# A two-layer Fourier and MLP kernel in float32: w3 and raw w4 loads at later steps, one product moved, norms a slot behind additions, six places for w4 tiles

## The chip, the cores and the metric

The kernel runs on one core of a Trainium2 chip. The metric is the device time of one execution, in microseconds (us). The engines of the core are named as in the profile: PE (TensorE, matrix products), DVE (VectorE), ACT (ScalarE), POOL (GpSimd) and SP (SyncE, which here issues all DMAs).

## The reference

The input `x` has 2048 tokens of 512 features, in float32. Two layers are computed, each in two sublayers that add to `x`:

```python
x = x + fourier(layernorm(x))      # Real(DFT_seq(DFT_hidden(.)))
x = x + mlp(layernorm(x))

def mlp(x):
    h  = gelu(layernorm(x) @ w1)            # 512 x 512
    hs = shift_tokens(h) @ w2               # four feature quarters by +1, -1, +2, -2
    x1 = x + hs
    return x1 + gelu(layernorm(x1) @ w3) @ w4   # 512 -> 1376 -> 512
```

## The kernel before

**Numbers and products.** Each float32 operand is split into a high part (a cast on ACT) and a low part (a subtraction on DVE); a product is three matmuls, high by high, high by low, low by high (`mm3`, lines 305 to 307). So every operand costs an ACT cast and a DVE "low" before TensorE can use it, and all three matmul lines look alike in the profile.

**Tiles.** The tokens stand in four chunks of 512 (`NC`), a chunk in four tiles of 128. The 1376 hidden features make eleven tiles (`NF`), numbered `fs` = 10, 0, 1, ... 9. Chunks 0 and 1 are worked as one pair, chunks 2 and 3 as the second. For h = gelu(z w3), two feature tiles and two chunks are a block product of 2 by 2, done in seven products instead of eight (`prod`, line 771) with sums of blocks named "11", "21", "12", "22", "t1" to "t4". Five such steps (p = 0 to 4) cover feature tiles 0 to 9; tile 10 is done by itself before (`w3x`).

**First pair** (in `by_pairs`, from line 1413). Each step p: seven products; two w4 tiles of the step before (`w4_part`, twelve matmuls each) for chunk c1; then after the last step two more tiles, and eleven tiles for chunk c2 (line 1532). w4 tiles come into six places `w4r`; after each tile the load that follows six tiles later is issued (`w4_load`). In layer 0 the steps also prepare the weights for all later uses (`w_prep`, line 1449): sums of w3, high and low parts, and stores of them in DRAM (`w3d`, `w3e`, `w4a`). Work that isn't bound to a place, the norms and transposes of chunks 2 and 3 for the second pair (z3), stands in a list `bg`, of which one entry, a slot, is run at each call of `one()`: two slots before step 0, two in step 0 and three in each later step of layer 0. The last entry stores z3 of chunk 3 (`turn_out`, line 616, four DMAs), and four loads (`b_in`, line 764) bring z3 back as blocks.

**Bank reuse in a step.** Block 11's product goes to bank b1; ACT copies it to `u` (line 1473); only then may block 21's product add to the same bank. Product t3 goes to bank b7, which is the bank b5 of the step before; there the last reader was that step's last addition.

**Second pair, layer 0** (`second_pair`, line 1286). Again tile 10, five steps and then 22 w4 tiles (eleven for each chunk). Beside the steps the first layer's raw w4 is brought in (`q4_raw`), summed for layer 1 (`q4_sums`, DVE, then a cast on ACT), its lows taken (`q4_lows`, DVE) and stored (`q4_keep`, DMA). These stand at five points of a step (`work`, line 1325). The w4 tiles come through six places `wq`, of which places 0 and 1 are used once. During the last eleven tiles the next layer's DFT blocks are brought into four places `raw` (`more`, line 1311) and made ready (`ahead`, line 289).

**Order.** The schedule is by hand: each engine runs its instructions in the order in which the program gives them, SP's DMAs among them. A DMA whose wait isn't over holds up all DMAs behind it on SP.

Of the kernel before, what the change touches and what calls it, by code (L numbers as in the profile page):

```python
# [8 lines left out]
F32 = mybir.dt.float32  # L9
# [25 lines left out]
WARM = 12  # L35

X6, X7 = 2, 4
HAT = (2, 3, 3, 4, 5, 5, 6, 6)
BACK = {1: (0,), 2: (2,), 6: (4,)}
HORDER = ((1, 0), (0, 1), (1, 1), (0, 0))  # L40
# [3 lines left out]
def spectral_mlp_kernel(ctx: ExitStack, tc: tile.TileContext, x, ws, hs, w1, w2, w34, out, out_t):  # L44
# [80 lines left out]
    extra = [at(f"extra{i}", EXT + i * D, D, dtype=F32) for i in range(6)]  # L125
    rest = [at(f"rest{i}", RAWS + i * D, D, dtype=F32) for i in range(8)]

    w4c, w4cf = zip(*(both(f"w4c{i}", word, 2, 4, 2 * P) for i, word in enumerate((6 * AY, 7 * AY, RNG))))
    w4raw = [at(f"w4raw{i}", RAWS + i * 2 * CH, 2, CH, dtype=F32) for i in range(2)]
    row_at = [ZW + i * CH for i in range(NF + 4)] + [RR + (8 + i) * CH for i in range(NF - 4)]  # L130
    hrow = [at(f"hrow{i}", word, CH, dtype=F32) for i, word in enumerate(row_at)]
    wq_at = [4 * CH, 6 * CH] + [RR + i * 2 * CH for i in range(4)]
    wq = [at(f"wq{i}", word, 2, CH) for i, word in enumerate(wq_at)]
    hp_at = [STG] + [RNG + (8 + 2 * i) * CH for i in range(3)] + [EXT + 2 * i * CH for i in range(3)]
    hp = [at(f"hp{i}", word, 2, CH) for i, word in enumerate(hp_at)]
# [647 lines left out]
            nc.sync.dma_start(to[:, 0], w34[NF - 1 + LAG, :, 1])  # L783

    def q4_sums(n):
        lo, w = w4cf[n % 3][:, 1], w4c[n % 3]
        (a11, a21), (a12, a22) = ([w4raw[n % 2][:, f, e * 2 * P : (e + 1) * 2 * P] for e in range(2)] for f in range(2))
        if n < NF // 2:
            add(lo[:, 1], a21, a22)
            add(lo[:, 3], a11, a21, ALU.subtract)  # L790
            add(lo[:, 2], lo[:, 1], a11, ALU.subtract)
            add(lo[:, 0], a12, lo[:, 2], ALU.subtract)
            nc.scalar.copy(w[:, 0], lo)
        else:
            add(lo[:, 0], a11, a21, ALU.subtract)
            add(lo[:, 1], a21, a11, ALU.subtract)
            nc.scalar.copy(w[:, 0, 0:2], lo[:, 0:2])

    def q4_lows(n):
        w, lo, u = w4c[n % 3], w4cf[n % 3][:, 1], slice(0, 4 if n < NF // 2 else 2)  # L800
        nc.vector.tensor_tensor(w[:, 1, u], lo[:, u], w[:, 0, u].bitcast(F32), op=ALU.subtract)

    def q4_keep(n):
        w = w4c[n % 3].bitcast(F32)
        if n < NF // 2:
            nc.sync.dma_start(w4s[:, n], w)
        else:
            nc.sync.dma_start(w4e, w[:, :, 0:2])

    def by_pairs(layer, zs, xin, dst):  # L810
# [147 lines left out]

        def w3_keep(n):
            nc.sync.dma_start(w3d[n], w3b[n % 2].bitcast(F32))  # L960

        sc0, sc1, sc2 = scratch
        for c in range(NC):
# [322 lines left out]
        def second_pair():  # L1286
# [19 lines left out]
                    nc.sync.dma_start(w_of(m).bitcast(F32), w4d[tiles[m][1]])  # L1306

            def w_of(m):
                return wq[m if m < 2 else 2 + (m - 2) % 4]

            def more():
                state.update(limit=w_items[1], load=len(pieces))
                issue_dma()

            s = w3xs[1][0]
            for c, names in ((c1, ("11", "21")), (c2, ("12", "22"))):
# [7 lines left out]

            def work(p):
                todo = {
                    0: [lambda: q4_sums(p)],
                    1: [lambda: xp_stats(p)] if p < half - 1 else [lambda: split_of(1)],
                    2: [lambda: q4_lows(p)],
                    3: [lambda: xp_norm_in(p)] if p < half - 1 else [lambda: split_of(2)],  # L1330
                    4: [lambda: q4_keep(p), lambda: q4_raw(p + 2) if p + 2 <= half else None],
                }
                if p == 1:
                    todo[3].append(lambda: split_of(0))
                if p == half - 1:
                    todo[2] += [lambda: load(0), lambda: load(1)]
                    todo[4].append(lambda: split_of(3))
                return todo

# [36 lines left out]
            def store(c):  # L1376
# [7 lines left out]
                NF: [lambda: drain(c1, acc4), lambda: store(c1)],  # L1384
                NF + 1: [lambda: xp_stats(4)],
                NF + 2: [lambda: xp_stats(5), lambda: xp_norm_in(4)],
                NF + 3: [lambda: xp_norm_in(5), more],
            }
            for m in (NF + 5, NF + 7, NF + 9):
                plan[m] = [lambda: ahead(1)]  # L1390
            for k, first in enumerate((0, 3, 6, 9, NF + 3, NF + 6)):
                for i, f in enumerate((xp_sums, xp_highs, xp_lows)):
                    plan.setdefault(first + i, []).append(lambda f=f, k=k: f(k))

            for m, (c, f) in enumerate(tiles):
                if m == NF:
                    for g in plan.pop(m):
                        g()
                acc, h, w = acc4 if c == c1 else mm4, splits.pop(m), w_of(m)
                split_of(m + 3) if m else None  # L1400
                for q in range(TC):
                    v = slice(q * P, (q + 1) * P)
                    mm3(acc[q], h[:, 0, v], h[:, 1, v], w[:, 0], w[:, 1], f == fs[0], f == fs[-1])
                if m >= 2:
                    load(m + 4)
                for g in plan.pop(m, ()):
                    g()
            assert not plan
# [4 lines left out]
        for pair in range(NC // 2):  # L1413
# [4 lines left out]
            bk, acc1 = (mm4, acc4) if pair == 0 else (acc4, mm4)  # L1418
            acc2 = [bk[i] for i in (3, 0, 1, 2)]
            if pair == 0:  # L1420
                bg += [] if layer else [lambda: None] * 2 + [u_stats(2, 0), u_stats(2, 2)]
                bg += [finish(2, 0), finish(2, 2), turn3(turned, 2, 0, 1), turn3(turned, 2, 2, 3)]
                bg += [lambda: turn_out(turned, z3d[2])]
                z3_last = lambda t: [
                    *(u_stats(3, 0), u_stats(3, 2), finish(3, 0), finish(3, 2)),
                    *(turn3(t, 3, 0, 1), lambda: (turn3(t, 3, 2, 3)(), turn_out(t, z3d[3]))),
                ]
                bg += z3_last(turned if layer else tmp[:, 0:4])
            tmps[:] = gs
            lows("t4")()  # L1430
            if layer == 0:
# [17 lines left out]
            def w_prep(p):  # L1449

                n, i = p + 1, 2 * p + 1
                w4_lows = lambda: (w4_low(i), w4_low(i + 1))
                w4_highs = lambda: (w4_high(i), w4_high(i + 1))
                if n == NF // 2:
                    return {1: [w4_highs], 5: [w4_lows]}
                return {
                    0: [lambda: w3_sums(n, 0), lambda: w3_highs(n, 1, 2)],
                    1: [lambda: w3_sums(n, 1), lambda: w3_highs(n, 0)],
                    2: [lambda: w3_lows(n, 1, 2), *([lambda: w3_load(n + 1)] if n < NF // 2 - 1 else [])],
                    3: [w4_highs],  # L1460
                    4: [lambda: w3_lows(n, 0), lambda: w3_keep(n)],
                    5: [w4_lows],
                }

            b1, b6, b5, b7 = bk[2], bk[3], bk[0], bk[1]
            for p in range(NF // 2):
                prep = {} if layer else w_prep(p)
                u, v, x, y = sets[p % 2]
                w = w3b[(5 * pair + p) % 2]
                if p:  # L1470
                    b1, b5, b7 = b7, b1, b5
                prod(b1, w, 4, "11")
                nc.scalar.copy(u, b1)
                at_point(0)
                prod(b6, w, 1, "t2")
                add(x, u, b6)
                prod(b5, w, 0, "t1")
                if layer:
                    one()
                at_point(1)  # L1480
                prod(b1, w, 5, "21", True)
                low1 = gelu_high(h4[2 * (p % 2)], b1)
                at_point(2)
                prod(b7, w, 2, "t3")
                add(v, x, b7)
                add(y, v, b5)
                gelu(hc[:, 2 * p + 1], y)
                if layer:
                    one()
                low1()  # L1490
                at_point(3)
                tiles = [(fs[0], h4[2])] if p == 0 else [(2 * p - 2 + i, h4[2 * ((p - 1) % 2) + i]) for i in range(2)]
                for i, (f, h) in enumerate(tiles):
                    w4_part(acc1, f, h, lambda: at_point(4 + i))
                    w4_load()
                    one()
                at_point(4)
                at_point(5)
                if p == NF // 2 - 1:
                    split_later(0)  # L1500
                    split_later(1)
                prod(b1, w, 6, "t4")
                add(v, v, b1)
                low2 = gelu_high(h4[2 * (p % 2) + 1], v)
                prod(b5, w, 3, "22", True)
                add(x, x, b5)
                low2()
                gelu(hc[:, 2 * p], x)
                at_point(6)
                if layer or p >= NF // 2 - 2:  # L1510
                    w3_load(5 * pair + p + 2)
                one()

            if pair == 0:
# [2 lines left out]
                        b_in(c, half, to)  # L1517
                bg += [sum_of("t1", "12", "11"), sum_of("t2", "22", "t1"), sum_of("t3", "22", "12"), sum_of("t4", "21", "t2")]
                bg += [parts(b) for b in ("11", "21", "12", "22", "t2", "t1", "t3", "t4")]
            if layer == 0:  # L1520
                nc.sync.dma_start(w3xs[1][0].bitcast(F32), w3e)
                q4_raw(0)
                q4_raw(1)
            for i in range(2):
                w4_part(acc1, NF - 3 + i, h4[i])
                w4_load()
# [5 lines left out]
            for k in range(NF):  # L1532
                w4_part(acc2, fs[k], h4[(2 + k) % 4])
                w4_load()
                if k:
                    split_later(k + 3)
                one()
            drain(c2, acc2)
            for j in range(c2 * TC, c2 * TC + TC, 2):
# [216 lines left out]
```

## Time and profile before

| | us |
|---|---|
| three runs | 1454.46, 1454.02, 1451.78 |
| median | 1454.02 |
| the profiled execution | 1454.86 |
| its span, first to last instruction | 1452.7 |
| mean granted TensorE clock | 0.996 |

The stretch that the change touches, by the trace of before, in us from the span's start: the steps of the first pair in layer 0 run from 505.6 to 581.7, the w4 tiles behind them to 628, the steps of the second pair from 633 to 682 and its w4 tiles to 745. A row of the list of waits reads: who waited, on whom, us in total, how many times, the longest. A row of the timeline reads: start, duration, engine, line, operation, tiles written and read, count, and in brackets the idle time before it and what ended it. A row of the windows reads: window, its length, then for PE, weight loads, DVE, ACT and POOL the busy time and instructions, then granted clock, DMA share and GB/s. A row of the chain reads: start, us, what.

### The profile page before, as it was taken

What the parts mean: (1) busy time and instruction counts of PE and PEld (TensorE: products, weight loads), DVE (VectorE), ACT (ScalarE), POOL (GpSimd) and SP (SyncE); (2) the same over time, 40 slices, a digit from 0 to 9 for tenths busy, and PEclk for the clock granted to TensorE, in tenths of its full rate; (3) what the DMA queues carried; (4) which work ended last, traced back from release to release, by engine and by line L of the source; (5) the groups of instructions that cost most, each with busy time, mean ns of one, the idle gap of its engine ahead of it and who ended that gap; (6) DMA issues with size and microseconds to landing.
All of it is one profiled execution on the core that took longest, in us unless ns stands there. A gap on an engine that the chain in (4) does not pass through costs nothing.

```text
span 1452.7 us, 17322 instructions
## 1 busy us (share of the span) xinstructions
PE 1431.3 (99%) x6290; PEld 1179.4 (81%) x6290; DVE 1142.9 (79%) x1598; ACT 726.6 (50%) x983; POOL 78.5 (5%) x111
## 2 busy tenths in 40 slices
PE   9999999999999999799999999999999999999998
PEld 8888888888888887687877888888888888888887
DVE  7876997998869887467889978979978698636585
ACT  5563454454556654245545534544546566433352
POOL 2100000000001000000000000000000010000000
PEclk9999999999999999899999999999999999999999
DMA  7326556557546759939755466565575459656594
GB/s 250 127 89 210 194 188 202 190 184 250 189 132 154 266 212 328 335 119 331 237 200 179 166 203 203 174 200 205 165 263 196 132 131 331 198 194 246 170 311 148
DMA packets 131533, 297.93 MB, mean 205 GB/s; under 512 B 15212, under 2 KB 56940, under 8 KB 128248
## 3 DMA queue, kind: packets, MB, share of 16 engines
q1 hardware_dynamic: 131448, 296.83, 61.3%
q8 instruction: 49, 0.80, 0.2%
q14 instruction: 36, 0.29, 0.1%
HBM read 244.08 MB, written 52.72 MB: 204 GB/s over the span
## 4 chain that ended last, share of the span: by engine, by line
PE 87%; DVE 6%; DMA 5%; ACT 1%; issue 1%; POOL 0%; SPq 0%; DVEq 0%; ACTq 0%; POOLq 0%
PE psd L305 10%; PE psd L307 10%; PE psd L306 10%; PE psa L305 8%; PE psa L307 8%; PE psa L306 8%; PE psc L305 6%; PE psc L306 6%; PE psc L307 6%; PE psb L306 6%; PE psb L307 6%; PE psb L305 6%; DMA w4raw<-in_w 2%; DMA wq<-w4a 1%; DVE ring L268 1%
## 5 line engine op out<-in xcount | busy, mean ns | idle before, releaser
L251 ACT CAST ring<-raw 128x1024 fp32r<-128x1024 f32 x127 | 133.0, 1052 | 103.9 <-PE psd L307 52.3
L268 DVE TENSOR_TENSOR ring<-raw,ring 128x1024 fp32r<-128x1024 f32 (+1 forms) x128 | 154.7, 1212 | 25.5 <-ACT ring L251 25.5
L307 PE MATMUL psd<-ring,rr 128*128 128x512 f32 x208 | 81.0, 390 | 0.0
L305 PE MATMUL psd<-ring,rr 128*128 128x512 f32 x208 | 81.0, 390 | 0.0
L306 PE MATMUL psd<-ring,rr 128*128 128x512 f32 x208 | 81.0, 390 | 0.0
L345 POOL TENSOR_TENSOR rs<-ve,mhalf 128x4 f32<-128x4 f32 x16 | 28.7, 1793 | 610.0 <-DVE nm L344 610.0
L258 ACT CAST ring<-ring0f 128x1024 fp32r<-128x1024 f32 x28 | 29.5, 1054 | 54.9 <-DVE ring0f L257 54.9
L268 DVE TENSOR_TENSOR ring<-ring1f,ring 128x512 fp32r<-128x512 f32 (+1 forms) x56 | 53.3, 952 | 0.7 <-ACT ring L254 0.7
L324 POOL TENSOR_TENSOR rs<-ve,mhalf 128x2 f32<-128x2 f32 (+1 forms) x33 | 29.4, 890 | 417.4 <-DVE nb L323 417.4
L306 PE MATMUL psb<-ring,ay 128*128 128x512 f32 x128 | 50.0, 391 | 0.5 <-DVE ring L268 0.5
L305 PE MATMUL psc<-ring,ay 128*128 128x512 f32 x128 | 50.0, 391 | 0.3 <-ACT rr11f L500 0.3
L306 PE MATMUL psc<-ring,ay 128*128 128x512 f32 x128 | 50.0, 391 | 0.0
L305 PE MATMUL psb<-ring,ay 128*128 128x512 f32 x128 | 49.9, 390 | 0.0
L307 PE MATMUL psc<-ring,ay 128*128 128x512 f32 x128 | 49.9, 390 | 0.0
L307 PE MATMUL psb<-ring,ay 128*128 128x512 f32 x128 | 49.9, 390 | 0.0
L305 PE MATMUL psa<-ring,ay 128*128 128x512 f32 x126 | 49.1, 390 | 0.0
L305 PE MATMUL psd<-ring,ay 128*128 128x512 f32 x126 | 49.1, 390 | 0.0
L307 PE MATMUL psa<-ring,ay 128*128 128x512 f32 x126 | 49.1, 390 | 0.0
L307 PE MATMUL psd<-ring,ay 128*128 128x512 f32 x126 | 49.1, 390 | 0.0
L306 PE MATMUL psd<-ring,ay 128*128 128x512 f32 x126 | 49.1, 390 | 0.0
L306 PE MATMUL psa<-ring,ay 128*128 128x512 f32 x126 | 49.1, 389 | 0.0
L258 ACT CAST ring<-ring1f 128x1024 fp32r<-128x1024 f32 x28 | 29.5, 1055 | 37.3 <-DVE ring1f L257 37.3
(579 smaller groups left out, 4388.4 us busy)
## 6 DMA issues: line engine op xcount, KB each, us to landing
raw<-in_ws SPq DMA_DIRECT2D x183, 512.0 KB, 4.9
raw<-in_hs SPq DMA_DIRECT2D x56, 512.0 KB, 3.6
w3b<-w3d SPq DMA_DIRECT2D x15, 1792.0 KB, 7.7
w4r<-w4a SPq DMA_DIRECT2D x33, 512.0 KB, 7.5
wq<-w4a SPq DMA_DIRECT2D x22, 512.0 KB, 4.8
w3d<-w3b SPq DMA_DIRECT2D x5, 1792.0 KB, 6.7
x1d<-tmp SPq DMA_DIRECT2D x12, 512.0 KB, 7.6
xs<-x1d SPq DMA_DIRECT2D x12, 512.0 KB, 6.6
```

The lines of the kernel that those rows point to most:

```text
L251: nc.scalar.copy(dest[:, a:b, 0], r[0][:, a:b])
L258: nc.scalar.copy(dest[:, :, 0], lo)
L268: nc.vector.tensor_tensor(lo[:, i], src[:, i], hi[:, i].bitcast(F32), op=ALU.subtract)
L305: nc.tensor.matmul(o, lh, rh, start=first, stop=False, skip_group_check=onto)
L306: nc.tensor.matmul(o, lh, rl, start=False, stop=False, skip_group_check=onto)
L307: nc.tensor.matmul(o, ll, rh, start=False, stop=last, skip_group_check=onto)
L324: nc.gpsimd.tensor_tensor(rs[:, :n], ve[:, :n], mhalf[:, 0, :n], op=ALU.pow)
L345: nc.gpsimd.tensor_tensor(rs, ve, mhalf[:, :, :2], op=ALU.pow)
```

## The change

It has six parts, all in layer 0's MLP but for the second and third, which both layers run.

1. The w3 load for the second pair's step 1 goes out at tile k = 7 of chunk c2 and not at the end of step 4; the raw w4 loads 0 and 1 at k = 5 and k = 9 and not ahead of the last w4 tiles; the load of `w3e` at the begin of step 4.
2. In a step of the first pair, product t3 with its two additions stands ahead of block 21's product.
3. `finish`, which added and normed two tiles in one slot, becomes an addition in one slot and the norm in the next, where the next addition or the transposes stand as well. The store of chunk 2's z3 moves a slot forward; the list keeps its length in layer 0.
4. In the second pair `q4_raw` stands at point 0, behind the sums, and `q4_lows` at point 4, ahead of the keep. The sums alternate between two places for the first five, so the third is used once.
5. The `wq` places 0 and 1 move and are used by the first twelve tiles in turn with the other four; a load is issued six tiles ahead for these, four ahead for later ones. Loads 0 and 1 are issued at point 0 of step 4.
6. The DFT loads go out one at a time, at tiles 12, 14, 16 and 18, and not four at tile 14; `ahead` comes a tile later (17, 19, 21), and the first of the sums for the next layer one tile later.

```diff
+QW = (0, 1, 0, 1, 0, 2)
-    w4c, w4cf = zip(*(both(f"w4c{i}", word, 2, 4, 2 * P) for i, word in enumerate((6 * AY, 7 * AY, RNG))))
+    w4c, w4cf = zip(*(both(f"w4c{i}", word, 2, 4, 2 * P) for i, word in enumerate((6 * AY, 7 * AY, RNG + 4 * CH))))
-    wq_at = [4 * CH, 6 * CH] + [RR + i * 2 * CH for i in range(4)]
+    wq_at = [RNG, RNG + 2 * CH] + [RR + i * 2 * CH for i in range(4)]
...
+        def both_of(*fs):
+            return lambda: [f() for f in fs]
...
             def w_of(m):
-                return wq[m if m < 2 else 2 + (m - 2) % 4]
+                return wq[m % 6 if m < 12 else 2 + m % 4]
             def more():
                 state.update(limit=w_items[1], load=len(pieces))
-                issue_dma()
+                issue_dma(state["dma"] + 1)
...
                 todo = {
-                    0: [lambda: q4_sums(p)],
+                    0: [lambda: q4_sums(p), lambda: q4_raw(p + 2) if p + 2 <= half else None],
                     1: [lambda: xp_stats(p)] if p < half - 1 else [lambda: split_of(1)],
-                    2: [lambda: q4_lows(p)],
+                    2: [],
                     3: [lambda: xp_norm_in(p)] if p < half - 1 else [lambda: split_of(2)],
-                    4: [lambda: q4_keep(p), lambda: q4_raw(p + 2) if p + 2 <= half else None],
+                    4: [lambda: q4_lows(p), lambda: q4_keep(p)],
                 }
                 if p == half - 1:
-                    todo[2] += [lambda: load(0), lambda: load(1)]
+                    todo[0] += [lambda: load(0), lambda: load(1)]
...
-                NF + 3: [lambda: xp_norm_in(5), more],
+                NF + 3: [lambda: xp_norm_in(5)],
             }
-            for m in (NF + 5, NF + 7, NF + 9):
+            for m in range(NF + 1, NF + 8, 2):
+                plan.setdefault(m, []).append(more)
+            for m in (NF + 6, NF + 8, NF + 10):
                 plan[m] = [lambda: ahead(1)]
-            for k, first in enumerate((0, 3, 6, 9, NF + 3, NF + 6)):
+            for k, first in enumerate((1, 3, 6, 9, NF + 3, NF + 6)):
...
-                if m >= 2:
-                    load(m + 4)
+                if m < 6 or m >= 8:
+                    load(m + (6 if m < 6 else 4))
...
-                bg += [finish(2, 0), finish(2, 2), turn3(turned, 2, 0, 1), turn3(turned, 2, 2, 3)]
-                bg += [lambda: turn_out(turned, z3d[2])]
...
+                def z3_of(c, t):
+                    return [
+                        *(add_u(c, 0, 1), both_of(norm3(c, 0, 1), add_u(c, 2, 3))),
+                        both_of(norm3(c, 2, 3), turn3(t, c, 0, 1)),
+                        both_of(turn3(t, c, 2, 3), lambda: turn_out(t, z3d[c])),
+                    ]
+                bg += z3_of(2, turned) + [u_stats(3, 0)] + ([] if layer else idle) + [u_stats(3, 2)] + z3_of(3, t)
...
                 if n == NF // 2:
-                    return {1: [w4_highs], 5: [w4_lows]}
+                    return {0: [lambda: nc.sync.dma_start(w3xs[1][0].bitcast(F32), w3e)], 1: [w4_highs], 5: [w4_lows]}
...
                 at_point(1)
+                prod(b7, w, 2, "t3")
+                add(v, x, b7)
+                add(y, v, b5)
                 prod(b1, w, 5, "21", True)
                 low1 = gelu_high(h4[2 * (p % 2)], b1)
                 at_point(2)
-                prod(b7, w, 2, "t3")
-                add(v, x, b7)
-                add(y, v, b5)
...
-                if layer or p >= NF // 2 - 2:
+                if layer or p == NF // 2 - 2:
                     w3_load(5 * pair + p + 2)
...
-            if layer == 0:
-                nc.sync.dma_start(w3xs[1][0].bitcast(F32), w3e)
-                q4_raw(0)
-                q4_raw(1)
...
+                if layer == 0:
+                    {5: lambda: q4_raw(0), 7: lambda: w3_load(NF // 2 + 1), 9: lambda: q4_raw(1)}.get(k, idle[0])()
```

More of the change, by code (lines that the diff above doesn't have):

```diff
@@ L785, in q4_sums @@
     def q4_sums(n):
-        lo, w = w4cf[n % 3][:, 1], w4c[n % 3]
+        lo, w = w4cf[QW[n]][:, 1], w4c[QW[n]]
         (a11, a21), (a12, a22) = ([w4raw[n % 2][:, f, e * 2 * P : (e + 1) * 2 * P] for e in range(2)] for f in range(2))
@@ L799, in q4_lows @@
     def q4_lows(n):
-        w, lo, u = w4c[n % 3], w4cf[n % 3][:, 1], slice(0, 4 if n < NF // 2 else 2)
+        w, lo, u = w4c[QW[n]], w4cf[QW[n]][:, 1], slice(0, 4 if n < NF // 2 else 2)
         nc.vector.tensor_tensor(w[:, 1, u], lo[:, u], w[:, 0, u].bitcast(F32), op=ALU.subtract)
     def q4_keep(n):
-        w = w4c[n % 3].bitcast(F32)
+        w = w4c[QW[n]].bitcast(F32)
         if n < NF // 2:
@@ L1420, in by_pairs @@
             if pair == 0:
-                bg += [] if layer else [lambda: None] * 2 + [u_stats(2, 0), u_stats(2, 2)]
-                bg += [finish(2, 0), finish(2, 2), turn3(turned, 2, 0, 1), turn3(turned, 2, 2, 3)]
-                bg += [lambda: turn_out(turned, z3d[2])]
[L1424 to L1428, printed above, removed]
+                def z3_of(c, t):
[4 more added lines that the diff above has]
+                    ]
+                t = turned if layer else tmp[:, 0:4]
+                idle = [lambda: None]
+                bg += [] if layer else idle * 2 + [u_stats(2, 0), u_stats(2, 2)]
+                bg += z3_of(2, turned) + [u_stats(3, 0)] + ([] if layer else idle) + [u_stats(3, 2)] + z3_of(3, t)
             tmps[:] = gs
```

## The prediction

> **What bounds the kernel now.** I read the page first, then who TensorE waits for, then that stretch in narrow windows.
>
> ```profile
> PE 1431.3 (99%) x6290; PEld 1179.4 (81%) x6290; DVE 1142.9 (79%) x1598; ACT 726.6 (50%) x983; POOL 78.5 (5%) x111
> PE   9999999999999999799999999999999999999998
> ...
> PE psa L305 <- DMA w4r<-w4a: 8.7, 1, 8.7
> PE psd L305 <- ACT rest L1473: 3.4, 2, 2.8
> PE psd L305 <- DMA wq<-w4a: 1.6, 1, 1.6
> ...
> PE psd L305 <- DVE rest L475: 0.5, 1, 0.5
> ...
> PE psc L305 <- DMA wq<-w4a: 0.4, 1, 0.4
> ...
> PE psb L305 <- DVE rest L475: 0.3, 1, 0.3
> ```
>
> TensorE is busy for 1431.3 of 1452.7 us, so no edit that leaves the matmuls alone can win more than 21. One matmul takes 1431.3 / 6290 = 0.2276 us; a product of six takes 1.37, a w4 tile of twelve 2.73. The waits that the change can reach are the six above, 8.7 + 3.4 + 1.6 + 0.5 + 0.4 + 0.3 = 14.9 us, all in the stretch from 530 to 740 us; the same loops in layer 1 show none. The dent in the slices is the 8.7. A loss that the list of waits doesn't show lies behind it:
>
> ```profile
> 569.00:572.00 3.00, 1.31 (x6) 1.09 (x7) 0.84 (x2) 2.68 (x5) 0.00 (x0) 1.00 1.02 412
> ...
> 597.00:600.00 3.00, 1.19 (x6) 0.65 (x4) 0.00 (x0) 0.62 (x1) 0.00 (x0) 1.00 1.04 396
> 600.00:603.00 3.00, 0.00 (x0) 0.00 (x0) 2.67 (x3) 1.04 (x1) 0.00 (x0) 0.59 1.06 397
> ...
> 609.00:612.00 3.00, 3.00 (x11) 2.33 (x11) 0.00 (x0) 0.52 (x1) 0.00 (x0) 0.71 1.03 419
> ...
> 585.93 10.30 DMA w3b<-w3d
> 596.29 10.45 DMA w4r<-w4a
> 606.88 0.76 PE psa L305
> ```
>
> The third number from the end is the granted clock. TensorE falls idle at 597 + 1.19 = 598.19. A clock of 0.59 in 600 to 603 is half clock from 600.54 on, and 0.71 in 609 to 612 is half clock up to 610.74. Work resumed at 606.88, so 3.86 us of it ran at half speed: 1.93 us lost. The one wait costs 8.69 + 1.93 = 10.6 us.
>
> **First pair, the late w4 tile.** The chain (last three rows) says how the load got late: its issue waited for the end of an older DMA, and then it took 10.45 us behind others. The SP queue shows which:
>
> ```profile
> 579.55 6.28 SPq L624 DMA_DIRECT2D z3d<-tmp  x4
> 585.93 0.95 SPq L931 DMA_DIRECT2D w3b<-w3d  x1
> ...
> 588.98 1.16 SPq L765 DMA_DIRECT2D b12f<-z3d  x1
> ...
> 590.88 2.20 SPq L1521 DMA_DIRECT2D w3x<-w3e  x1
> 593.12 1.73 SPq L781 DMA_DIRECT2D w4raw<-in_w  x2
> 596.29 1.71 SPq L902 DMA_DIRECT2D w4r<-w4a  x2
> ...
> w3b<-w3d SPq DMA_DIRECT2D x2, 1792.0 KB, 12.2
> w4raw<-in_w SPq DMA_DIRECT2D x2, 512.0 KB, 11.4
> ```
>
> Ahead of the w4 load stood the w3 load (1792 KB) and two raw w4 loads (1024 KB) that go to later steps, and the w3e load (512 KB) that goes to the last step's begin: 3.41 MB, 8.6 us at the 397 GB/s of the window row. What then remains ahead of it is the way of z3: transposes, four stores, the four b loads. I follow it in the new order, on the clock of before. Both waits on the copy at L1473 vanish (next part), so TensorE is 3.4 us early here: the step ends near 578 and tile 15, which stalled, is wanted at 598.19 - 3.4 = 594.8. The stores start at 579.55 - 3.4 = 576.1 and are issued by 582.4. In before b12f's issue came 588.98 - 585.83 = 3.15 us after the stores' issue ended (it reads what they write): 585.6, and with one more 512 KB ahead of the stores nearer 586. Two loads then go out ahead of the w4 load, which is issued at about 588. Four b loads and itself are 5 x 0.52 MB from 586 on, 1.3 us each at 400 GB/s: it lands at 593, **1.8 us before it is wanted**. The next ones come 1.3 us apart and two 512 KB stores lie between; tile 17 lands at 598, wanted at 600.2. VectorE, which stood still for 11.09 us until b12f landed at 600.24, starts the sums near 590.5 and reaches the split of tile 15 at 592. So all 10.6 us go. The moved loads are wanted late: the first raw w4 and the w3 were first used at 629.8 and 642.8, so near 616 and 629 now, and they go out at 600 to 611, behind the last w4 load.
>
> **First pair, block 21 and the norms.** The longer wait on the copy:
>
> ```profile
> 534.91 0.68 DVE L475 TENSOR_TENSOR rest<-rest,psa 128x512 f32<-128x512 f32 x1
> ...
> 564.53 1.53 ACT L353 ACTIVATE rest<-rest,nb,rs 128x512 f32<-128x512 f32 x2 [1.54 <-POOL nb L325]
> ...
> 568.65 1.52 ACT L353 ACTIVATE rest<-rest,nb,rs 128x512 f32<-128x512 f32 x2 [0.89 <-DVE xs L745]
> 570.07 0.56 ACT L1473 COPY rest<-psd 128x512 f32<-128x512 f32 x1
> ```
>
> ScalarE stood 0.89 us for an addition, did two norms and only then made the copy that frees the bank to which block 21's product adds: 570.63, where the product was due at 570.69 - 2.83 = 567.86. Now t3's product stands ahead of it, so it is due 1.37 us later, and 0.57 earlier with the other wait gone: 568.7. In this slot stand norms whose additions were done a slot before. By these rows alone (free at 567.76, then 1.52 and 0.56) the copy would still end at 569.8 and 1.1 us would stay. But the slot before loses its own pair of norms and their wait, 1.54 + 1.53, and these held the gelus ahead of the copy: some 2.5 us earlier, near 567. I take nothing; bounds 0 and 1.1. In step 2 (3.4 - 2.8 = 0.6) the norms come right ahead of the copy: it ends within 0.3 us of the new due time on either side, and I take nothing there too. t3's bank must first be read by the last addition of the step before. The tightest is step 2: that addition ends at 535.59, and t3's new place is where block 21's stood, 537.1; so 1.5 us are left and it costs nothing. VectorE's new order also fills a wait for ScalarE's cast with two additions, which only makes it earlier. Where the cover goes, this part costs its 3.4 again. Sum: -3.4.
>
> **Second pair.** Four waits (0.3, 0.5, 0.4, 1.6) go for sure or probably: the raws arrive a step earlier, so VectorE no longer stands 2.72 us in step 4, and the four raw DFT loads that went out at once now go out singly:
>
> ```profile
> 675.60 0.76 DVE L475 TENSOR_TENSOR w4c1f<-w4raw 128x256 f32<-128x256 f32 x2 [2.72 <-DMA w4raw<-in_w]
> ...
> 724.41 2.09 SPq L233 DMA_DIRECT2D raw<-in_ws  x4
> 726.76 5.76 SPq L1306 DMA_DIRECT2D wq<-w4a  x3
> ```
>
> But `q4_lows` moves from point 2 to point 4, behind the step's last addition, and the store `q4_keep` with it. Two costs follow.
>
> Step 2, VectorE:
>
> ```profile
> 654.48 0.69 DVE L674 TENSOR_TENSOR hp<-hrow,hp 128x512 fp32r<-128x512 f32 x1 [2.62 <-DMA w4raw<-in_w]
> 655.09 0.68 DVE L475 TENSOR_TENSOR tmp<-tmp,psa 128x512 f32<-128x512 f32 x1
> ...
> 660.21 0.69 DVE L475 TENSOR_TENSOR rest<-rest,psb 128x512 f32<-128x512 f32 x1
> 660.82 1.22 DVE L801 TENSOR_TENSOR w4c<-w4c2f,w4c 128x1024 fp32r<-128x1024 f32 x1
> 661.95 0.68 DVE L475 TENSOR_TENSOR rest<-rest,psd 128x512 f32<-128x512 f32 x1
> ```
>
> The split at 654.48 waits for ScalarE's cast (a load named there had nothing to do with it), so VectorE is late and works on without a gap; the addition at 660.21 is the one that block 22's product waits for (the 0.3). Now the lows of step 1, 1.13 us from start to start, stand between 655.09 and there: the wait is 0.3 + 1.13 = **1.43**. Bounds 0.3 to 2. In steps 3 and 4 the same order leaves 0.6 us or more.
>
> Behind step 4:
>
> ```profile
> 682.01 0.32 SPq L806 DMA_DIRECT2D w4s<-w4c  x1
> 682.42 14.74 SPq L1306 DMA_DIRECT2D wq<-w4a  x7
> ...
> 683.74 0.69 DVE L674 TENSOR_TENSOR hp<-hrow,hp 128x512 fp32r<-128x512 f32 x1 [1.21 <-ACT hp L677]
> 684.35 0.68 DVE L475 TENSOR_TENSOR rest<-rest,psd 128x512 f32<-128x512 f32 x1
> ...
> 688.37 0.47 PE psc L305
> ```
>
> SP issues in order, and the loads of w4 tiles 2 to 5 stand right behind the last keep. In before the keep went at 682.01 and tile 2, wanted at 687.97, started at 688.37: 6.36 us from keep to use. Now VectorE first splits hp (683.3, once ScalarE has cast), adds (to 684.5) and does the lows of 1.22: the keep goes out at 685.75, tile 2 can start at 692.1 and is wanted at about 688.0: a new wait of **4.0 us**. If ScalarE's cast comes early it is 2.9, if late as in the row above 4.8. The six places bring nothing there: tiles 0 and 1 are issued in step 4 (behind its keep of step 3; lands 681.4, wanted 682.6), tile 6 on come behind tiles 2 to 5.
>
> Does 4.0 us lower the clock? The rows bracket it: a wait of 2.83 us (567.86 to 570.69) left it at 1.00, the 8.69 one lowered it after 2.35. I take the row with the drop, as 4.0 is beyond the 2.35: **1.93** more. The Trainium skill, "TensorE: Matmul & The Clock Gate", What's actually happening, says that the gate halves the clock after a wholly idle window of about 3.4 us of a free-running count. The trace disagrees in so far as the drop came 2.35 us after the last work. By that rule a 4.0 us wait would mostly not lower the clock, and the sum would be 1.93 less.
>
> **Sum**, against the profiled execution, 1454.86 us (span 1452.7 and 2.2 around it): -10.62 - 3.40 - 2.81 + 1.43 + 4.0 + 1.93 = -9.5, that is 1445.4. The median of the runs is 0.84 lower; from it 1444.5. I forecast **1444.5**.
>
> **Rivals.**
> - The clock stays (a wait of 2.83 us left it alone): 1442.6. Chance 0.15. The rule of the Trainium skill above would give the same.
> - The keep doesn't hold the tiles, because VectorE is through early or the loads overtake: only 1.43 is new, 1454.0 - 16.8 + 1.4 = 1438.6. Against it: the seven loads at 682.42 start right behind the keep, as in the program. 0.12.
> - The late w4 tile is only half cured: the slack of 1.8 us rests on z3's stores and on DMA engines that are full (share 1.02 to 1.06). 2 to 6 us of it stay, with the clock: 1446.5 to 1451. 0.15.
> - Slower: the transposes of z3's last chunk, now one slot behind their norms on ScalarE, come late; b12f waits for their stores, and the w4 load stands behind b12f on SP. It costs from 1.8 us of lateness on, and at 12 the whole 10.6 is back: 1454.0 - 3.4 - 2.8 + 1.4 + 4.0 + 1.9 = 1455.2, with the upper ends of the new waits 1457. Against it: ScalarE has gaps of 1.5 us there. 0.04.
> - The change doesn't do what it says at the end of the second pair: a w4 load there has a lead of three tiles as before (the six places hold for the first twelve tiles alone), and the raws delay it though they go out singly. The 1.6 stays: 1446.1. 0.04.
>
> My forecast has 0.50, its own range 1443.4 to 1445.9 by the bounds of the new waits. The range of 1438.0 to 1449.5 leaves out the slower case and the edges of two others, under 0.2. A difference of 0.2% (2.9 us) is about what can be told from no change: faster 0.94, same 0.03, slower 0.03.
>
> **What would show it.** Right: no wait on w4r and none on the copy at L1473; the clock at 1.00 near 600; a wait of about 4 us on wq at tile 2 of the second pair, with a keep right before on SP and a dip of the clock; some 1.4 us on VectorE's addition in step 2; none on wq near the end. Wrong: a w4r wait that b12f's landing precedes closely (the slack was misjudged), or no wait at tile 2 (then VectorE was faster than I count).

## The result and the profile after

| | before | after |
|---|---|---|
| median, four runs each | 1454.24 (1451.78 to 1454.46) | 1443.20 (1442.94 to 1443.45) |
| span of the profiled execution | 1452.7 | 1441.2 |
| time of that execution | 1454.86 | 1442.94 |

The ratio is 0.9928 (0.9911 to 0.9945), or 11.0 us less by the medians. From the page of the changed kernel, the busy times and the slices of TensorE; then who TensorE waits for:

```profile
PE 1429.3 (99%) x6290; PEld 1178.6 (82%) x6290; DVE 1144.2 (79%) x1598; ACT 725.9 (50%) x983; POOL 79.7 (6%) x111
PE   9999999999999999998999999999999999999998
```
```profile
PE psc L306 <- DMA wq<-w4a: 4.0, 1, 4.0
PE psb L306 <- DVE rest L476: 1.4, 1, 1.4
PE psd L161 <- POOL mhalf L58: 1.4, 1, 1.4
PE psb L307 <- DVE ring L269: 0.4, 1, 0.4
PE psc L306 <- ACT rr11f L501: 0.3, 1, 0.3
```

The counts of instructions are as before and TensorE is busy 2 us less. The dent of the slices has moved from about 600 us to about 680 and is shallower. The row on w4r (8.7) and the row on the copy (3.4) are gone, as are the two on wq (1.6 and 0.4) and the 0.5 on an addition; a row of 4.0 on wq is new, and the one of 0.3 on VectorE's addition has grown to 1.4. (The lines have moved by one or more: L305 to L307 are now L306 to L308.)

**First pair.** SP's queue of the changed kernel, the addition that waited for b12f, and two windows of the stretch in which TensorE had waited and run at half clock:

```profile
575.84 5.55 SPq L625 DMA_DIRECT2D z3d<-tmp  x4
581.43 0.99 SPq L766 DMA_DIRECT2D b11f<-z3d  x1
582.46 1.15 SPq L766 DMA_DIRECT2D b21f<-z3d  x1
584.95 0.36 SPq L766 DMA_DIRECT2D b12f<-z3d  x1
585.41 0.42 SPq L766 DMA_DIRECT2D b22f<-z3d  x1
585.87 0.94 SPq L903 DMA_DIRECT2D w4r<-w4a  x2
```
```profile
590.28 1.23 DVE L476 TENSOR_TENSOR bt1f<-b12f,b11f 128x1024 f32<-128x1024 f32 x1 [4.75 <-DMA b12f<-z3d]
```
```profile
594.00:597.00 3.00, 3.00 (x15) 2.49 (x14) 3.00 (x4) 1.57 (x2) 0.00 (x0) 1.00 1.06 420
...
600.00:603.00 3.00, 3.00 (x15) 2.49 (x14) 2.11 (x3) 1.86 (x3) 0.00 (x0) 1.00 0.99 398
```

Behind the b loads the w4 loads follow at once: at 585.87, where they had gone out at 596.29. TensorE is busy for all of both windows at full clock.

**Second pair.** VectorE in step 2, then behind step 4, SP there, and the windows of tile 2:

```profile
639.98 0.69 DVE L675 TENSOR_TENSOR hp<-hrow,hp 128x512 fp32r<-128x512 f32 x1 [2.62 <-ACT hp L678]
640.59 0.68 DVE L476 TENSOR_TENSOR tmp<-tmp,psa 128x512 f32<-128x512 f32 x1
641.19 1.22 DVE L802 TENSOR_TENSOR w4c<-w4c1f,w4c 128x1024 fp32r<-128x1024 f32 x1
...
646.85 0.69 DVE L476 TENSOR_TENSOR rest<-rest,psb 128x512 f32<-128x512 f32 x1
...
668.87 0.69 DVE L675 TENSOR_TENSOR hp<-hrow,hp 128x512 fp32r<-128x512 f32 x1 [1.21 <-ACT hp L678]
669.47 0.68 DVE L476 TENSOR_TENSOR rest<-rest,psd 128x512 f32<-128x512 f32 x1
670.07 1.22 DVE L802 TENSOR_TENSOR w4c<-w4c0f,w4c 128x1024 fp32r<-128x1024 f32 x1
```
```profile
671.35 0.32 SPq L807 DMA_DIRECT2D w4s<-w4c  x1
671.77 16.41 SPq L1310 DMA_DIRECT2D wq<-w4a  x9
```
```profile
677.77 0.47 PE L306 MATMUL psc<-wq,hp 128*128 128x512 f32 x1 [4.04 <-DMA wq<-w4a]
```
```profile
673.00:676.00 3.00, 0.73 (x4) 0.27 (x2) 0.33 (x1) 1.14 (x2) 0.00 (x0) 1.00 0.96 265
676.00:679.00 3.00, 1.23 (x5) 1.06 (x6) 2.23 (x4) 1.47 (x3) 0.00 (x0) 0.98 1.03 421
679.00:682.00 3.00, 3.00 (x8) 2.31 (x7) 0.00 (x0) 0.63 (x2) 0.00 (x0) 0.50 1.02 416
682.00:685.00 3.00, 3.00 (x14) 2.43 (x13) 2.48 (x4) 0.57 (x2) 0.00 (x0) 0.95 0.96 318
```

The chain is split, addition, lows, keep, loads, tile. The lows end at 671.29, SP issues the keep at 671.35 and the loads behind it, and tile 2 starts 677.77 - 671.35 = 6.42 us after the keep (6.36 in before). The clock's column shows that the drop came after work had resumed at 677.77: 3 x (0.02 + 0.50 + 0.05) = 1.7 us lost.

Matmul for matmul against the profile of before, TensorE's lateness changes so:

| place | us |
|---|---|
| the two waits on the copy | -3.7 |
| w4r, wait and half clock | -10.8 |
| addition of step 2 | +1.1 |
| addition of step 4 | -0.7 |
| tile 2 on wq | +3.6 |
| half clock behind it | +1.6 |
| wq near the end | -1.7 |
| layer 1, small steps | -0.8 |
| all | -11.4, of 11.5 in the spans |

About 0.6 of the -0.8 also appears at the same place in loads_alone below, which leaves layer 1 as it was; that much belongs to the one profiled execution of before and not to the change.

### The profile page after: what moved, and what is told of

Same layout as the page of the kernel before. It is cut to its first block, busy times and chain, and to the rows that moved or that the text cites. A ratio compares the mean times of both kernels' runs of the same rounds, so it can differ in the third digit from the quotient of the medians.

```text
span 1441.2 us, 17321 instructions
## 1 busy us (share of the span) xinstructions
PE 1429.3 (99%) x6290; PEld 1178.6 (82%) x6290; DVE 1144.2 (79%) x1598; ACT 725.9 (50%) x983; POOL 79.7 (6%) x111
## 4 chain that ended last, share of the span: by engine, by line
PE 95%; DVE 3%; DMA 1%; ACT 1%; issue 0%; POOL 0%; SPq 0%; DVEq 0%; ACTq 0%; POOLq 0%
PE psd L306 11%; PE psd L308 10%; PE psd L307 10%; PE psa L307 9%; PE psa L306 9%; PE psa L308 9%; PE psc L306 6%; PE psc L308 6%; PE psc L307 6%; PE psb L307 6%; PE psb L306 6%; PE psb L308 6%; DVE ring L269 1%; DMA raw<-in_ws 1%; DMA wq<-w4a 0%
## 5 line engine op out<-in xcount | busy, mean ns | idle before, releaser
L308 PE MATMUL psd<-ring,rr 128*128 128x512 f32 x208 | 80.9, 389 | 0.0
L307 PE MATMUL psd<-ring,rr 128*128 128x512 f32 x208 | 80.9, 389 | 0.0
L306 PE MATMUL psd<-ring,rr 128*128 128x512 f32 x208 | 80.9, 389 | 0.0
L307 PE MATMUL psb<-ring,ay 128*128 128x512 f32 x128 | 49.9, 390 | 0.4 <-DVE ring L269 0.4
L306 PE MATMUL psc<-ring,ay 128*128 128x512 f32 x128 | 49.9, 390 | 0.3 <-ACT rr11f L501 0.3
L307 PE MATMUL psc<-ring,ay 128*128 128x512 f32 x128 | 49.9, 390 | 0.0
L308 PE MATMUL psc<-ring,ay 128*128 128x512 f32 x128 | 49.8, 389 | 0.0
L306 PE MATMUL psb<-ring,ay 128*128 128x512 f32 x128 | 49.8, 389 | 0.0
L308 PE MATMUL psb<-ring,ay 128*128 128x512 f32 x128 | 49.8, 389 | 0.0
L307 PE MATMUL psa<-ring,ay 128*128 128x512 f32 x126 | 49.0, 389 | 0.0
L306 PE MATMUL psd<-ring,ay 128*128 128x512 f32 x126 | 49.0, 389 | 0.0
L306 PE MATMUL psa<-ring,ay 128*128 128x512 f32 x126 | 49.0, 389 | 0.0
L308 PE MATMUL psd<-ring,ay 128*128 128x512 f32 x126 | 49.0, 389 | 0.0
L308 PE MATMUL psa<-ring,ay 128*128 128x512 f32 x126 | 49.0, 389 | 0.0
L307 PE MATMUL psd<-ring,ay 128*128 128x512 f32 x126 | 49.0, 389 | 0.0
```

The costliest lines, as they stand in the source:

```text
L306: nc.tensor.matmul(o, lh, rh, start=first, stop=False, skip_group_check=onto)
L307: nc.tensor.matmul(o, lh, rl, start=False, stop=False, skip_group_check=onto)
L308: nc.tensor.matmul(o, ll, rh, start=False, stop=last, skip_group_check=onto)
```

## The experiments

The theory: the gain is two cures, that of the late w4 load (moved loads) and that of the copy (block 21's place and the norms), and 7.2 us are lost because the lows and the keep behind them now stand late (1.4 on the addition, 4.0 + 1.7 on tile 2; by the table 6.3 more than before lost at these places). The rivals are that one cure alone brings the other, that the norms bring nothing, and that tile 2 is late through the keep's bytes or through fewer places for w4. Each kernel is timed against the kernel before on its own chip.

### One part alone, or one undone

**loads_back**: the changed kernel with the loads where they were.

```diff
-                    return {0: [lambda: nc.sync.dma_start(w3xs[1][0].bitcast(F32), w3e)], 1: [w4_highs], 5: [w4_lows]}
+                    return {1: [w4_highs], 5: [w4_lows]}
-                if layer or p == NF // 2 - 2:
+                if layer or p >= NF // 2 - 2:
+            if layer == 0:
+                nc.sync.dma_start(w3xs[1][0].bitcast(F32), w3e)
+                q4_raw(0)
+                q4_raw(1)
-                if layer == 0:
-                    {5: lambda: q4_raw(0), 7: lambda: w3_load(NF // 2 + 1), 9: lambda: q4_raw(1)}.get(k, idle[0])()
```

> The changed kernel with its first part undone: the w3 load of step 1, both raw w4 loads and the w3e load go out ahead of the last w4 tiles again, as before. Theory (these 3.41 MB held the w4 tile): TensorE waits again on w4r<-w4a, 8.5 to 9.5 us at the fifth tile of chunk 2's eleven, with half clock after it, and the time is about 1453.5. Rival (the earlier stores of z3 and the norms cured it, the loads only shared the time): a wait under 3 us, time under 1447.

Measured 1452.16 against 1454.36 of before, ratio 0.9988 (0.9976 to 0.9999): nearly all of the gain is gone. The list of waits and SP's queue of this kernel:

```profile
PE psa L306 <- DMA w4r<-w4a: 7.2, 1, 7.2
```
```profile
585.84 1.86 SPq L1530 DMA_DIRECT2D w3x<-w3e  x1
587.74 1.74 SPq L782 DMA_DIRECT2D w4raw<-in_w  x2
590.71 1.70 SPq L903 DMA_DIRECT2D w4r<-w4a  x2
```

The wait is back with nothing else changed: w3e and the raws stand ahead of w4r again. It is 7.2 and not 8.7. The wait's place and cause held; its size was a little less than expected.

**loads_alone**: the kernel before with the moved loads and nothing else (the same lines the other way round).

> The kernel before with the first part of the change alone. Theory: the w4r wait of 8.7 us and its half clock go although the two waits on the copy at L1473 stay, time about 1443.6. Rival (the shift of 3.4 us in the steps was needed so that z3 is stored in time): 5 us or more of the wait stay, time above 1448.

Measured 1445.94 (three executions, 1442.97 to 1446.48), ratio 0.9936 (0.9906 to 0.9965). No wait on w4r is left, both waits on the copy stay. The median is 2.3 above the theory's number, and the windows say why:

```profile
PE psd L305 <- ACT rest L1473: 3.4, 2, 2.8
```
```profile
569.00:572.00 3.00, 1.33 (x3) 1.14 (x4) 0.82 (x2) 2.66 (x5) 0.00 (x0) 0.63 1.04 419
572.00:575.00 3.00, 3.00 (x8) 2.32 (x8) 0.00 (x0) 1.22 (x2) 0.00 (x0) 0.50 1.09 453
575.00:578.00 3.00, 3.00 (x11) 2.36 (x11) 1.77 (x3) 0.36 (x1) 0.00 (x0) 0.73 0.83 333
```

The same wait on the copy, 2.82 us here and 2.83 in before, this time lowered the clock, from 569.8 to 576.6. Work resumed at 570.67, so 5.9 us of it ran at half speed and about 3 were lost. These windows are of the execution of 1445.94, with a mean clock of 0.998; the fastest, 3.0 us shorter, had 1.000, the third (1446.48) 0.999. The mechanism of the loads held by itself; the clock's answer to a wait of this length is not fixed.

**block21_alone**: the kernel before with t3's product moved.

```diff
                 at_point(1)
+                prod(b7, w, 2, "t3")
+                add(v, x, b7)
+                add(y, v, b5)
                 prod(b1, w, 5, "21", True)
                 low1 = gelu_high(h4[2 * (p % 2)], b1)
                 at_point(2)
-                prod(b7, w, 2, "t3")
-                add(v, x, b7)
-                add(y, v, b5)
```

> The kernel before with product t3 ahead of block 21's alone, norms as before. Theory (the due time moves 1.37 us later, ScalarE's copy does not move): the wait of 0.6 goes, the one of 2.8 falls to about 2.0 or less; time 0 to 1.4 less than before. Rival (the product's place alone cures both): no wait on the copy is left, time 3.4 less.

Measured 1449.78, ratio 0.9969 (0.9949 to 0.9989). Both waits on the copy are gone, where the theory had 2.0 left. VectorE of this kernel, then ScalarE:

```profile
553.61 1.40 DVE L475 TENSOR_TENSOR rest<-rest,psd 128x512 f32<-128x512 f32 x2
554.93 1.02 DVE L957 TENSOR_TENSOR w3b<-staged,w3b 128x512 fp32r<-128x512 f32 x2
```
```profile
566.30 1.52 ACT L353 ACTIVATE rest<-rest,nb,rs 128x512 f32<-128x512 f32 x2 [0.89 <-DVE xs L745]
567.73 0.56 ACT L1473 COPY rest<-psd 128x512 f32<-128x512 f32 x1
```

The copy still stands behind the 0.89 us wait and its two norms, yet it comes at 567.73 and not at 570.07: all of VectorE's work ahead of it is earlier. In before VectorE stood 1.17 us for ScalarE's cast ahead of the L957 row and did the additions of t3 afterwards; here the additions fill that wait, and L957 follows with none. The steps add up: instruction for instruction VectorE is 1.1 us earlier behind the first such wait, 2.2 behind the second and 2.35 ahead of the norms. The copy ends at 567.73 + 0.56 = 568.29, and the product, 1.37 later by its place and 0.57 earlier because the other wait is gone, is due at 568.66. The product's place alone cures the copy: the rival held.

**norms_alone**: the kernel before with the norms a slot behind the additions (`z3_of` as in the diff above).

> The kernel before with the norms a slot behind the additions alone, products in the old order. Theory (the copy of step 4 ends near 567.5, due at 567.9; in step 2 the norms stand right ahead of the copy): the wait of 2.8 falls under 0.5, the one of 0.6 grows to 1 to 1.7; time about 2 less than before. Rival (the norms alone cure both): no wait on the copy is left, time 3.4 less.

Measured 1452.34, ratio 0.998 (0.9968 to 0.9993). By the trace the short wait on the copy grew from 0.57 to 1.7 and the long one fell from 2.83 to 0.15:

```profile
PE psd L305 <- ACT rest L1479: 1.7, 1, 1.7
```

Alone, the norms move the wait from one step to another, since they now come right ahead of the copy in step 2. The wait on w4r is 7.0 here. The wait on wq near the end was longer in this execution, 2.5 and not 1.6, and half clock followed it from 735.5 to 738.9; why it grew no run shows.

**norms_undone**: the changed kernel with the list of norms and additions of before.

```diff
-                bg += z3_of(2, turned) + [u_stats(3, 0)] + ([] if layer else idle) + [u_stats(3, 2)] + z3_of(3, t)
+                bg += [finish(2, 0), finish(2, 2), turn3(turned, 2, 0, 1), turn3(turned, 2, 2, 3)]
+                bg += [lambda: turn_out(turned, z3d[2])]
...
+                bg += z3_last(turned if layer else tmp[:, 0:4])
```

> The changed kernel with the norms again in the slot of their additions (its third part undone). Theory, from the run of block 21's place alone (no wait on the copy was left there): the norms' place is worth nothing here, no wait on the copy over 0.3 us, a w4r wait of at most 1 us as the split-keep run had it, time within 1 of the changed kernel. Rival (the norms' place is needed once the loads are gone, for the copy or for the store of z3): 1.5 us or more of wait on the copy or on w4r, time above 1444.5.

Measured 1443.29, ratio 0.9923 (0.9906 to 0.9941), against 0.9928 (0.9911 to 0.9945) of the change: the same. A wait of 0.3 on the copy is all that comes back. Beside block 21's place the third part of the change is worth nothing that these runs can tell.

**dft_at_once**: the changed kernel with the four DFT loads at one tile.

```diff
-                issue_dma(state["dma"] + 1)
+                issue_dma()
-            for m in range(NF + 1, NF + 8, 2):
+            for m in (NF + 3,):
```

> The changed kernel with the four DFT loads issued at once at tile 14 again, ahead a tile later kept. Theory (four loads of 512 KB ahead of one w4 load hold its tile): a wait on wq of 1.2 to 2.5 us near the nineteenth tile comes back, time 1444.4 to 1446. Rival (the wait went for another reason, the later start of the ring's work or the phase of the tiles): no wait over 0.3 us in the last eleven tiles, time as the changed kernel, 1443.2.

Measured 1444.18, ratio 0.9933 (0.9915 to 0.9951). The wait on wq near the end is back:

```profile
PE psd L306 <- DMA wq<-w4a: 1.3, 1, 1.3
```

So, by the trace, the 1.6 of before came from four loads issued at once ahead of a w4 load with a lead of three tiles, and the single issue is what removed it. The ranges of the two kernels' times meet, so the times alone don't show it.

### What was given back

**lows_point2**: the changed kernel with the lows at point 2, where before had them.

```diff
-                    2: [],
+                    2: [lambda: q4_lows(p)],
-                    4: [lambda: q4_lows(p), lambda: q4_keep(p)],
+                    4: [lambda: q4_keep(p)],
```

> The changed kernel with q4_lows at point 2 of a step again, keep at point 4, raw load at point 0. Theory (the lows behind the last addition make both new waits): the wait on VectorE in step 2 falls from 1.44 to about 0.3, the one on wq at tile 2 from 4.0 to under 0.5, no half clock there; 1.1 + 3.7 + 1.6 less, time about 1436.6. Rival (the wait comes from the loads' place behind the keep and its 1024 KB, whenever the lows are done): 2 us or more stay at tile 2, time above 1439.

Measured 1436.39 (1435.85 to 1437.37), ratio 0.9865 (0.9851 to 0.988): 6.8 below the changed kernel's median, and neither the ranges nor the intervals of the ratios meet. Its waits, without the 1.4 at the kernel's start:

```profile
PE psb L306 <- DMA w3b<-w3d: 0.9, 1, 0.9
PE psc L306 <- ACT rr11f L501: 0.3, 1, 0.3
PE psb L306 <- DVE rest L476: 0.3, 1, 0.3
PE psc L306 <- DMA wq<-w4a: 0.3, 1, 0.3
```

The addition's wait is at 0.3 again, tile 2's too, and the clock stays at 1.00. A wait of 0.9 on a w3 load is new: the next thing that comes late when these go.

**tiles_first**: the changed kernel, lows still at point 4, with the loads of tiles 2 to 5 ahead of the last keep.

```diff
+                if p == half - 1:
+                    for m in range(2, 6):
+                        load(m)
                 at_point(4)
-            for m in range(2, 6):
-                load(m)
```

> The changed kernel with the loads of w4 tiles 2 to 5 ahead of the last step's keep on SP. Theory: the wait at tile 2 and its half clock go (4.0 + 1.6), the 1.44 in step 2 stays, time about 1437.6. Rival (VectorE's late lows hold tile 2's split too): 2 us or more stay at tile 2 and are then put down to VectorE, time above 1440.

Measured 1436.97 (1436.37 to 1437.55), ratio 0.9868 (0.9852 to 0.9884). The 1.4 on the addition stays, the wait at tile 2 and the half clock are gone. The places of w4 are as in the changed kernel, so they are not what made tile 2 late.

**lows2_tiles_first**: both of these edits.

> Both edits in the changed kernel, lows at point 2 and the four loads ahead of the last keep. Theory: neither new wait is left but some 0.3 in step 2, time 1436.2 to 1436.6, the fastest of all. Rival (one of the two moves a transfer into the way of another, the last raw or the sums of the last product): a new wait of 1 us or more in the 22 tiles, time above 1437.5.

Measured 1436.69 (1436.33 to 1437.66), ratio 0.9868 (0.9853 to 0.9882). The three versions aren't told apart: their ranges lie over each other. Any of them beats both kernels.

**low_half_first** and **half_keep** part the keep's wait from its bytes. The last keep is stored in two halves, one ahead of the loads of tiles 2 to 5 and one behind. The low half is what `q4_lows` writes; the high half is ready earlier.

```diff
+            def q4_half(p, i):
+                nc.sync.dma_start(w4s[:, p, i], w4c[QW[p]].bitcast(F32)[:, i])
...
-                    4: [lambda: q4_lows(p), lambda: q4_keep(p)],
+                    4: [lambda: q4_lows(p), lambda: q4_keep(p) if p < half - 1 else q4_half(p, 1)],
...
             for m in range(2, 6):
                 load(m)
+            q4_half(half - 1, 0)
```

This is low_half_first; half_keep has 0 and 1 exchanged, so that the high half goes first.

> The changed kernel with the last step's keep split: the high half (512 KB) is stored ahead of the loads of tiles 2 to 5, the low half behind them. All theories: the wait at tile 2 falls by the time of 512 KB, from 4.0 to 2.8 us. On the clock. Theory (the clock is lowered when about two thirds of a fixed window of 3.4 us are idle, and the windows lie anywhere): a wait of 2.8 us lowers it in some executions and not in others, so single times spread over 1440.3 to 1442.2. Rival (a wait under 3.4 us never lowers it): all times near 1440.3.

> The changed kernel with the last step's keep split the other way: its low half (512 KB, which waits for the lows) ahead of the loads of tiles 2 to 5, the high half behind them. All theories: SP waits for the lows as in the changed kernel, but 512 KB less go ahead, so the wait at tile 2 is 4.0 - 1.3 = 2.8 us. On the clock. Theory (the clock is lowered when some two thirds of a window of about 3.4 us are idle, and the windows lie anywhere): lowered in some executions and not in others, single times spread over 1440 to 1442.2. Rival (a wait under 3.4 us never lowers it): all times near 1440, no half clock after tile 2.

half_keep measured 1436.91 (1436.42 to 1437.42), ratio 0.9881 (0.9864 to 0.9899), and the wait at tile 2 was gone, where 2.8 had been expected by all. SP's queue of it:

```profile
664.42 0.32 SPq L1330 DMA_DIRECT2D w4s<-w4c  x1
665.29 3.68 SPq L1310 DMA_DIRECT2D wq<-w4a  x4
672.36 0.32 SPq L1330 DMA_DIRECT2D w4s<-w4c  x1
```

The expectation had overlooked that the high half needs no lows: SP issued it at 664.42 and the loads right behind, 6.5 us ahead of the changed kernel's. It tells the two causes apart all the same. With 512 KB of the keep ahead of them and no wait, the tiles are in time. As there was no wait, this run says nothing of the clock.

low_half_first measured 1442.22 (1441.44 to 1443.28), ratio 0.9916 (0.9898 to 0.9933). Here SP waits for the lows as in the changed kernel and half of the bytes are gone from the way:

```profile
PE psc L306 <- DMA wq<-w4a: 3.0, 1, 3.0
```
```profile
676.00:679.00 3.00, 2.44 (x7) 2.00 (x8) 0.00 (x0) 0.00 (x0) 0.00 (x0) 0.72 1.01 294
679.00:682.00 3.00, 3.00 (x11) 2.37 (x10) 0.00 (x0) 0.00 (x0) 0.00 (x0) 0.72 0.99 392
```

So half of the keep's bytes are 1.06 of the 4.04 us. In both kernels 512 KB go ahead of the loads, and only where SP stands for the lows does tile 2 wait, 2.98 us against none: bytes add to the wait, the stand makes it. With all the bytes ahead but the lows done early (lows_point2) 0.3 was left. And 3.0 us of waiting lowered the clock here, again after work had resumed: 3 x (0.28 + 0.28) = 1.7 us, so the rival that a wait under 3.4 us never lowers it is out. That single executions differ was expected as well, but is only hinted at: the fastest of the four (1441.44) had a mean clock of 1.000 and the profiled one (1442.23) 0.998, but the slowest (1443.28) 0.999.

## Why the prediction was right

**Size and sign.** 1444.5 was forecast and 1443.2 came, 0.2 below the forecast's own range and inside the wide one. Its terms, -9.5 in all, came out as -11.4; the difference is spread over small sizes and partly no part of the change (0.6 in layer 1). The bound of 21 us ahead of it left out that busy time shrinks too where half clock goes (1431.3 to 1429.3).

**The late w4 tile.** Right: -10.6 forecast, -10.8 measured, loads_alone and loads_back show it from both sides. VectorE's sums were to start near 590.5 and started at 590.28. What was mis-sized is the slack: 1.8 us were counted. In half_keep, with the same code up to there, the list of waits has this tile:

```profile
PE psa L306 <- DMA w4r<-w4a: 1.0, 1, 1.0
```

Its load went out at 586.36, earlier than the 588 that were counted, but its tile started only at 595.24, 8.9 us later, where the working had 5 us from issue to landing. The two errors cancel in part, and it is luck that the changed kernel shows no wait here: its tile, wanted at 594.31, had the load out at 585.87. The cure is real, but its margin is near zero, and the rival of the half-cured tile had more for it than the result alone lets one see.

**The copy.** -3.4 forecast, -3.7 measured, but the step's reason is only half right. It let the norms' new slot bring the copy forward by 2.5 us and named VectorE's filled wait as something that "only makes it earlier". block21_alone and norms_undone show otherwise: the filled wait and the product's later due time are enough without the norms. The norms do bring that copy forward (norms_alone: 2.83 to 0.15), but lengthen the other wait, and beside the product's place they add nothing that a time shows. The 1.1 us that the working named as its upper bound came from leaving the copy at its old time, which VectorE's filled waits undid.

**The waits given back.** The addition of step 2 was to cost 1.43 and cost 1.44; tile 2 was to wait 4.0 and waited 4.04. Both came from laying the moved instruction into the engine's order as the rows of before had it, and taking the interval from keep to use (6.36) as it stood. That the lows hold SP, and by it the tiles, is shown by lows_point2, half_keep and low_half_first together.

**The clock.** 1.93 was forecast, from the row with the drop, and 1.6 to 1.7 measured. The direction was right, the picture was not: the drop was placed 2.35 us into the wait, and came 1.1 us after work had resumed (678.9 against 677.77). That the sizes are near is luck: 1.93 was half of the 3.86 us that were left of a half clock of 10.2 us when work resumed, 1.7 is half of one whole stretch of 3.4. The rival that the clock stays was not met in this kernel.

**The end.** -1.6 forecast, -1.7 measured; dft_at_once shows the cause. The six places were forecast to bring nothing; no run undoes them alone, so that isn't shown.

**The rivals.** That the keep wouldn't hold the tiles (1438.6) did not happen in the change. Slower through z3's stores did not happen either: the four stores were issued by 581.4, a microsecond earlier than counted.

## What to carry to other kernels

On a queue that issues in order, look at each store for what it waits for and at what stands behind it: one store that waited for late work cost 4.0 us and then the clock, and moving four independent loads ahead of it gave all of it back. Loads that are wanted much later don't belong ahead of one that is wanted next: 3.41 MB of them were worth 10.8 us here, half clock included. Independent work put between the writing and the reuse of a bank helps twice, by a later due time and by filling another engine's waits, and where two edits are meant for one wait it pays to run each alone, since one of them may do it all.

## What the runs showed of the hardware

The clock's answer to a wait of about 3 us was not expected. A wait of 2.83 us left it at 1.00 in before, the same wait of 2.82 us halved it in loads_alone, 1.95 us after it began (567.85 to 569.80) and for 6.8 us; waits of 2.49 (norms_alone), 2.98 (low_half_first) and 4.04 (after) halved it only once work had resumed, for 3.4 us; that of 8.69 did so 2.35 us in, for 10.2 us. The lengths, 3.4, 6.8 and 10.2, are one, two and three times one length, 3.413 us.

The times between them are whole multiples of it too. loads_back has half clock twice, behind its waits on w4r and on wq; the end of the first and the begin of the second:

```profile
606.00:607.00 1.00, 1.00 (x5) 0.79 (x4) 0.00 (x0) 0.50 (x1) 0.00 (x0) 0.69 1.02 418
688.00:689.00 1.00, 1.00 (x5) 0.79 (x4) 0.38 (x1) 0.97 (x3) 0.00 (x0) 0.77 1.04 426
```

The clock is back at 606 + 2 x 0.31 = 606.62 and falls at 689 - 2 x 0.23 = 688.54, which is 81.92 us or 24 times 3.413 later. In norms_alone it is 126.3 us (609.2 to 735.5), 37 times. So within a run the clock changes on a beat of 3.413 us that no wait starts. Counting the beats back from each drop gives the share of a beat that TensorE spent waiting:

| kernel | wait | share of the beats in it | clock at their ends |
|---|---|---|---|
| before | 567.86 to 570.69 | 0.57, 0.26 | stays |
| loads_alone | 567.85 to 570.67 | 0.57 | falls |
| loads_back | 683.43 to 687.48 | 0.50, 0.69 | stays, falls |
| after | 673.73 to 677.77 | 0.52, 0.67 | stays, falls |
| norms_alone | 732.76 to 735.24 | 0.73 | falls |
| low_half_first | 673.58 to 676.56 | 0.09, 0.78 | stays, falls |
| before | 598.19 to 606.88 | 0.69 | falls |

In all the traces, eleven drops followed a wait: ten at the end of a beat of which 0.63 to 1.00 was waiting, one at 0.57. No beat at full clock with 0.52 or less ended in one, and at 0.57 both happened. So a mostly idle beat is enough, a wholly idle one isn't needed, and the place of a wait against the beat decides, besides its length. Where the edge lies between 0.52 and 0.63 isn't shown, nor can the beat's place be told ahead of a run. A wait of 3 us must be priced with the clock on both sides: 0 and 1.7 to 3 us.
